# Attention and gated MoE on one core: weight words, least scale and work order moved between engines

## The chip, the cores and the metric

The kernel runs on one core of a Trainium2 chip. The time is the device time of one execution in microseconds (us), and lower is better. Before the change the median of three runs is 902.36 us (901.72 to 904.81). The core has five engines with a queue each: PE multiplies matrices, DVE (VectorE), ACT (ScalarE) and POOL (GpSimd) work on tiles elementwise, and SP issues the DMAs.

## The reference

Four batches of eight heads, 768 positions of 64 numbers, then a gated MoE layer on the 3072 rows of 512 that come out:

```python
q_bits = (np.einsum('bhsd,dk->bhsk', q, proj) > 0)      # 6 bits, a bucket number
mask = q_bucket[:, :, :, None] == k_bucket[:, :, None, :]
scores = scale * np.matmul(q, k.transpose(0, 1, 3, 2))
scores = np.where(mask, scores, -1000000000.0)
attn = softmax(scores)                                  # with 1e-9 in the sum
x = np.matmul(attn, v)  # -> [3072, 512]
return (x @ w_a * (x @ w_b)) @ w_out                    # 512 -> 1536 -> 512
```

## The kernel before

Every fp32 operand is split into two fp16 numbers, hi and lo, and a product is three matmuls (hi*hi, lo*hi, hi*lo). The bucket test is part of the score matmul: 12 columns of marks stand beside the 64 of a key or query.

The scores are worked in 192 tiles of 128 queries by 768 keys. A tile goes through this chain: four matmuls `s` on PE, row maximum `mx` on DVE, `width` on DVE, `bias` on ACT (L1039) or DVE (L1045), exponential `e` on ACT, fp16 cast `a` (the hi half) on DVE, ACT (L1064) or POOL (L1065), the lo half `a` by subtraction on POOL (L1075) or DVE (L1079), one DMA transpose of both into `at` issued by SP (L1085), and 18 matmuls `av` on PE. Eight tiles make half a chunk of 256 rows; 12 chunks make the 3072 rows.

A chunk of x is divided by its sums and scaled by a power of two. The first and the last chunk are turned by PE: the two halves of x are scaled by `xsc` (L1215, POOL or DVE), transposed by PE into `px`, and split into `xT` hi (ACT L1241) and lo (DVE L1244). The ten chunks between go through DMA transposes. Then come the MoE matmuls `ab` (L1292), their product `g` (L1314, DVE), its split (hi L1322 ACT or L1326 DVE, lo L1334 POOL) and the matmuls `o` (L1344).

The weights come in as fp32 words in 18 pieces of 128x1024 (SP, L526), each into one of a few staging buffers `raw_w`, `raw_wo`. DVE takes group maxima (L624, L633), PE spreads them over the partitions, DVE reads the maximum (L585 `al_w`), raises it to at least 2^-14 (L599) and makes a power of two of it (L591, L594). A word is then split with integer steps: its hi part on ACT (L547), its low bits by a read of one byte in eight on ACT (L555), both put together by DVE (L562), which frees the staging buffer, and from that the fp16 hi (ACT L640) and lo (POOL L645 or DVE L649).

The order of everything is written out by hand. Each operation has a number, and the list `ORDER` names them in the order in which they are issued; +10000 or +20000 takes the operation's second or third engine, and a negative number -n puts n warming matmuls (`warm`, L1448) on PE that no result uses. An engine runs its instructions strictly in its own order; a semaphore holds an instruction back until what it reads is there and what it overwrites is done. So the engine of each operation and its place in each queue are set by this list alone.

Of the kernel before, what the change touches and what calls it, by code (L numbers as in the profile page):

```python
# [21 lines left out]
P = 128  # L22
# [21 lines left out]
SUMS = [1, 0]  # L44
# [31 lines left out]
def constants():  # L76
# [16 lines left out]

X_BY_PE = (0, NB * NCH - 1)
# [287 lines left out]
def attention_moe(ctx: ExitStack, tc: tile.TileContext, q, k, v, proj, w_a, w_b, w_out, cst, cst_w, out):  # L382
# [40 lines left out]
    veps = cp.tile([P, NB * NPAIR], F32, tag="veps", name="veps")  # L423
    wcut = cp.tile([P, NG], F32, tag="wcut", name="wcut")
    wone = cp.tile([P, NG + NFQ], F32, tag="wone", name="wone")
    wlow = cp.tile([P, NG], F32, tag="wlow", name="wlow")
    wtop = cp.tile([P, 2], F32, tag="wtop", name="wtop")
    wab = cp.tile([P, NPC, WP], F32, tag="wab", name="wab")
    wab16 = wab.bitcast(F16)
# [1057 lines left out]
```

## Time and profile before

| | before |
|---|---|
| median of three runs | 902.36 us |
| profiled execution | 903.96 us |
| its span | 902.2 us |
| PE busy | 859.0 us, 95% |
| DVE busy | 659.1 us, 73% |
| ACT busy | 544.4 us, 60% |
| POOL busy | 450.7 us, 50% |
| mean granted clock | 0.998 |

The span is the profiled execution without 1.76 us around it. "Busy" is time in an instruction, and a matmul that no result uses counts as well. A share of the whole span mixes two stages here, so the rows below are taken by stretch: the time up to 118.1 us, where the first MoE matmul begins, and the time behind it.

### The profile page before, as it was taken

The page shows a single profiled execution, that of the slowest core. Times are in us where ns is not written, and L with a number is a line of the kernel's source. Part 1 is how long each engine was busy: PE and PEld are TensorE (multiplying, and loading weights), DVE is VectorE, ACT ScalarE, POOL GpSimd, SP SyncE. Part 2 cuts the span into 40 slices and gives each one's busy share as a digit, 9 for nine tenths or more (in the row PEclk, how much of TensorE's full clock was granted, in tenths as well). Part 3 has the DMA queues.
Part 4 walks back from the last instruction along what each step waited for, and adds up shares of the span by engine and source line. Part 5 has one row for each costly group of instructions (what it writes and reads, how often), then busy time and mean ns, then how long its engine had stood idle before and what let it go on. Part 6 is the DMA issues. An engine that isn't in the chain of part 4 may idle for free.

```text
span 902.2 us, 23571 instructions
## 1 busy us (share of the span) xinstructions
PE 859.0 (95%) x9432; PEld 650.6 (72%) x9432; DVE 659.1 (73%) x1593; ACT 544.4 (60%) x1049; POOL 450.7 (50%) x388
## 2 busy tenths in 40 slices
PE   4787799999999999999999999999999999999998
PEld 3565577777777777777777777777777777777775
DVE  6999798988888769777876767777888854752310
ACT  5999799976555566556643555645566545543222
POOL 1478878886544373463533264573453545462111
PEclk9999999999999999999999999999999999999999
DMA  9899999999979999988979688997799966654000
GB/s 322 257 249 255 185 227 234 197 190 217 208 150 164 156 168 187 193 154 170 172 126 151 119 139 176 171 201 156 149 191 169 154 115 119 117 108 71 1 25 24
DMA packets 435950, 147.40 MB, mean 163 GB/s; under 512 B 407552, under 2 KB 428160, under 8 KB 435840
## 3 DMA queue, kind: packets, MB, share of 16 engines
q1 hardware_dynamic: 435840, 145.89, 83.2%
q8 instruction: 74, 1.21, 0.6%
q14 instruction: 36, 0.29, 0.1%
HBM read 37.85 MB, written 6.29 MB: 49 GB/s over the span
## 4 chain that ended last, share of the span: by engine, by line
PE 78%; DVE 4%; DMA 3%; ACT 2%; issue 1%; POOL 0%; ACTq 0%; SPq 0%; DVEq 0%
PE ab L1292 38%; PE o L1344 19%; PE s L1011 11%; PE av L1094 9%; DMA at<-a 2%; DMA qTA_q<-marked 1%; DVE mx L1023 1%; ACT e L1055 1%; DVE xz L1194 1%; DMA vr<-in_v_dram 1%; DVE g L1314 0%; PE b_q L802 0%; ACT raw_w L547 0%; ACT a L1064 0%; PE b_k L802 0%
## 5 line engine op out<-in xcount | busy, mean ns | idle before, releaser
L1292 PE MATMUL ab<-xT,wab 128*128 128x256 f16 x3456 | 407.8, 273 | 1.7 <-DVE g L1314 1.7
L1292 PEld LDWEIGHTS <-wab 128*128 128x128 f16 x3456 | 332.6, 98 | 55.8 <-issue 2.7
L1075 POOL TENSOR_TENSOR a<-e,a 128x768 f16<-128x768 f32 x148 | 249.9, 1693 | 107.9 <-ACT a L1064 53.5
L1055 ACT ACTIVATE e<-s,bias,width 128x768 f32<-128x768 f32 x192 | 189.8, 989 | 68.5 <-DVE bias L1045 58.3
L1334 POOL TENSOR_TENSOR g<-g,g 128x256 f16<-128x256 f32 x144 | 106.8, 742 | 234.9 <-ACT g L1322 151.0
L1344 PE MATMUL o<-wo,g 128*128 128x512 f16 x864 | 209.0, 379 | 0.0
L1023 DVE TENSOR_REDUCE mx<-s 128x1 f32<-128x768 f32 x192 | 181.6, 949 | 29.6 <-PE s L1011 29.0
L1314 DVE SCALAR_TENSOR_TENSOR g<-ab,wlow,a 128x256 f32<-128x256 f32 x132 | 63.5, 481 | 139.4 <-ACT a L1306 126.5
L1306 ACT ACTIVATE a<-ab,wlow 128x256 f32<-128x256 f32 x132 | 62.1, 471 | 158.7 <-PE ab L1292 151.9
L1094 PEld LDWEIGHTS <-at 128*128 128x128 f16 x3456 | 122.4, 98 | 28.2 <-DMA at<-a 9.7
L1344 PEld LDWEIGHTS <-g 128*128 128x128 f16 x864 | 81.2, 98 | 74.3
L1094 PE MATMUL av<-vh,at 128*128 128x64 f16 x2304 | 126.6, 194 | 6.9 <-DMA at<-a 6.9
L1011 PE MATMUL s<-kTA_k,qTA_q 128*128 128x384 f16 x384 | 94.2, 327 | 8.6 <-ACT e L1055 6.6
L1011 PE MATMUL s<-kTB_k,qTB_q 128*128 128x384 f16 x384 | 94.2, 327 | 0.0
L1065 POOL CAST a<-e 128x768 f16<-128x768 f32 x62 | 55.4, 895 | 58.8 <-ACT e L1055 47.9
L1064 ACT CAST a<-e 128x768 f16<-128x768 f32 x89 | 73.6, 829 | 5.8 <-DMA at<-a 4.4
L1094 PE MATMUL av<-vl,at 128*128 128x64 f16 x1152 | 65.3, 194 | 0.0
L1322 ACT CAST g<-g 128x256 f16<-128x256 f32 x102 | 40.9, 401 | 38.9 <-DVE g L1314 33.8
L1039 ACT ACTIVATE bias<-mx,width 128x1 f32<-128x1 f32 x101 | 29.3, 293 | 53.5 <-DVE width L1032 53.2
L1011 PEld LDWEIGHTS <-qTB_q 128*128 128x128 f16 x384 | 37.6, 98 | 25.2 <-issue 0.3
L1011 PEld LDWEIGHTS <-qTA_q 128*128 128x128 f16 x384 | 34.6, 98 | 28.3 <-issue 10.8
L1079 DVE TENSOR_TENSOR a<-e,a 128x768 f16<-128x768 f32 x44 | 42.8, 974 | 5.3 <-ACT a L1064 4.1
(149 smaller groups left out, 821.6 us busy)
## 6 DMA issues: line engine op xcount, KB each, us to landing
rk_k<-in_k_dram SPq DMA_DIRECT2D x16, 384.0 KB, 4.7
vr<-in_v_dram SPq DMA_DIRECT2D x16, 384.0 KB, 4.6
rq_q<-in_q_dram SPq DMA_DIRECT2D x12, 512.0 KB, 4.8
raw_w<-in_moe_w_b_dram SPq DMA_DIRECT2D x12, 512.0 KB, 5.2
raw_w<-in_moe_w_a_dram SPq DMA_DIRECT2D x12, 512.0 KB, 6.0
raw_wo<-in_moe_w_out_dram SPq DMA_DIRECT2D x12, 512.0 KB, 5.7
out_dram<-ob SPq DMA_DIRECT2D x24, 256.0 KB, 2.7
at<-a SPq DMA_TRANSPOSE x192, 4.1
```

Source lines behind the costliest of these rows:

```text
L1011: nc.tensor.matmul(ps.t[:, jj, :HALF], lhsT=x.t[:, uq, :], rhs=y.t[:, h * NT + jj * 3 : h * NT + jj * 3 + 3, :].rearrange("p t x -> p (t x)"),
L1023: lambda: nc.vector.tensor_reduce(out=mx.t[:, u : u + 1], in_=halves(ps.t), axis=AX.XY, op=ALU.max, negate=True),
L1055: lambda: nc.scalar.activation(flat2(e.t), halves(ps.t), AF.Exp, bias=bias.t[:, u : u + 1], scale=width.t[:, u : u + 1], accum_out=sm.t[:, ...
L1064: ("ACT", 0.725, lambda: nc.scalar.copy(out=a2.t[:, 0], in_=e.t), False),
L1065: ("POOL", 0.9, lambda: nc.gpsimd.tensor_copy(out=a2.t[:, 0], in_=e.t), False),
L1075: lambda: nc.gpsimd.tensor_tensor(out=a2.t[:, 1], in0=e.t, in1=a2.t[:, 0], op=ALU.subtract),
L1094: nc.tensor.matmul(av.t[:, u, :], lhsT=at.t[:, a + kt, :], rhs=w.t[:, h, kt, :], start=i == 0, stop=i == 3 * NT - 1,)
L1292: nc.tensor.matmul(pl.t[:, m, :CH], lhsT=wt(m, wi, cc, f), rhs=xt.t[:, :, xi * NC + cc, :], start=i == 0, stop=i == 3 * NC - 1,)
L1306: lambda a=a, pl=pl, gr=gr: nc.scalar.activation(a.t, pl.t[:, 0, :CH], AF.Copy, scale=cuts[:, gr : gr + 1]),
L1314: lambda a=a, g32=g32, pl=pl, gr=gr: nc.vector.scalar_tensor_tensor(out=g32.t, in0=pl.t[:, 1, :CH], scalar=cuts[:, gr + 1 : gr + 2], in1=a ...
L1334: lambda g=g, g32=g32: nc.gpsimd.tensor_tensor(out=g[1].t, in0=g32.t, in1=g[0].t, op=ALU.subtract),
L1344: nc.tensor.matmul(po.t[:, u, :], lhsT=g[gi].t[:, us], rhs=wo[f // 2].t[:, f % 2, wi * DM : (wi + 1) * DM], start=f % per_q == 0 and i == ...
```

## The change

The list `ORDER` is a new one (all 200 lines of it), and some operations get other engines to choose from:

- The low bits of a weight word (ACT) may also be taken on POOL, and the fp16 hi of a word (ACT or DVE) too. Five of the 18 low bits and one of the 18 hi casts go to POOL.
- The group maxima of the weights lie in one tile `wmx` that POOL fills with 2^-14 beforehand. Its last column is never written, so the reduce over the columns gives at least 2^-14, and the nine `max` instructions L599 go.
- `ident16`, the operand of the warming matmuls, is cast by POOL from `ident` instead of loaded; POOL clears `pjk` and `pjq`.
- The absolute sums of V and K heads may be taken by ACT with its accumulator, where DVE took a maximum.
- Counts that differ by engine: bias on ACT 101 to 84 and on DVE 91 to 108, sums and maxima of V and K heads on ACT 12 to 17 and on DVE 20 to 15, hi cast `a` on ACT 89 to 97, on DVE 41 to 42 and on POOL 62 to 53, lo `a` on POOL 148 to 144 and on DVE 44 to 48, x scaling on POOL 2 to 1 and on DVE 2 to 3, warming matmuls 318 to 315.

```diff
-SUMS = [1, 0]
+SUMS = [1, 1]
+    wmx = cp.tile([P, NG + NFQ, NC + 2], F32, tag="wmx", name="wmx")
-    op("SP", DMA_ISSUE, lambda: nc.sync.dma_start(out=ident16, in_=cst_w), -60, w=["ident16"], svc=0.3)
-    op("DVE", 0.1, lambda: nc.vector.memset(pjk, 0.0), -100, w=["pjk"])
+    op("POOL", 0.25, lambda: nc.gpsimd.tensor_copy(out=ident16, in_=ident), -60, ...
+    op("POOL", 0.1, lambda: nc.gpsimd.memset(pjk, 0.0), -100, w=["pjk"])
+    op("POOL", 0.1, lambda: nc.gpsimd.memset(wmx, float(2.0**-14)), -100, w=["wmx"])
...
+            alt=[(
+                "POOL", 1.1,
+                lambda: nc.gpsimd.tensor_scalar(
+                    out=low(), in0=raw.t.bitcast(U8)[:, :, 3], scalar1=1.0 / 32, scalar2=-15.5 / 32,
+                    op0=ALU.mult, op1=ALU.add,
+                ),
+                False,
+            )],
...
-            nc.vector.tensor_scalar(out=al.t, in0=al.t, scalar1=float(2.0**-14), scalar2=None, op0=ALU.max)
             power(sc.t, 0x7F800000, -1, 143 * 8)
...
-            lambda: nc.vector.tensor_reduce(out=mx.t[:, 0:1], in_=mx.t[:, 1:], axis=AX.X, op=ALU.max),
+            lambda: nc.vector.tensor_reduce(out=wmx[:, g, 0:1], in_=wmx[:, g, 1:], axis=AX.X, op=ALU.max),
...
-            alt=[("DVE", 0.6, lambda: nc.vector.tensor_copy(out=hi(), in_=z()), True)],
+            alt=[
+                ("DVE", 0.6, lambda: nc.vector.tensor_copy(out=hi(), in_=z()), True),
+                ("POOL", 1.05, lambda: nc.gpsimd.tensor_copy(out=hi(), in_=z()), False),
+            ],
-    6, 12, 0, 52, 60, 3, 2, 1, 40, 13, 296, 5, 299, 4, 14, 53, 300, 295, 15, 26, 16, 272, 61, 17, 273, 7, 276, 62,
+    1, 4, 5, 6, 7, 2, 13, 0, 53, 41, 61, 8, 297, 300, 301, 14, 9, 3, 296, 10, 274, 15, 16, 10054, 273, 17, 278, 11,
...
```

Three places of the order follow. The first is POOL from its first own instruction up to the first tiles, before (`marked` is the marks of a head pair, `a` and `e` belong to the score tiles):

```order
L441 MEMSET marked 128x16x52
L881 COPY marked<-nB_k_0_146 128x12x64
L881 COPY marked<-nB_q_0_176 128x16x64
L881 COPY marked<-nB_k_2_368 128x12x64
L1065 CAST a_0_0_0_0_0_0_521<-e_0_0_0_0_0_466 128x768
L1065 CAST a_0_0_0_0_0_1_530<-e_0_0_0_0_1_459 128x768
```

And the same place of the changed kernel, whose lines have other numbers (L898 is L881 of before, L568 the low bits, L657 the hi cast, L1083 is L1065):

```order
L446 MEMSET wmx 128x54
L448 MEMSET marked 128x16x52
L441 CAST ident_65<-ident 128x128
L898 COPY marked<-nB_q_0_170 128x16x64
L568 ISA
L568 TENSOR_SCALAR raw_w_1_127<-raw_w_1_127 128x1024
L568 TENSOR_SCALAR raw_w_0_138<-raw_w_0_138 128x1024
L568 TENSOR_SCALAR raw_w_1_153<-raw_w_1_153 128x1024
L898 COPY marked<-nB_k_2_397 128x12x64
L657 CAST wab<-wab 128x2x512
L1083 CAST a_0_0_0_0_0_0_517<-e_0_0_0_0_0_464 128x768
```

Three low bits stand between the copy for q and that for the head pair 2, and one hi cast ahead of the first tile; one copy and one cast of `a` have gone to DVE and ACT.

The second place is ACT at the scores of the sixth to eighth tile, before (`e_0_0_1_...` are tiles of the second half of eight, `raw_w` and `raw_wo` weight words):

```order
L1064 CAST a_0_0_0_1_0_1_917<-e_0_0_1_0_1_872 128x768
L1039 ACTIVATE bias_0_0_451<-mx_0_0_445,width_0_0_448 128x1
L555 ACTIVATE raw_w_0_591<-raw_w_0_591 128x1024
L1055 ACTIVATE e_0_0_1_1_0_961,sm_0_0_460<-s_0_0_1_1_0_867,bias_0_0_451,width_0_0_448 128x768
L1039 ACTIVATE bias_0_0_451<-mx_0_0_445,width_0_0_448 128x1
L1064 CAST a_0_0_0_1_1_0_986<-e_0_0_1_1_0_961 128x768
L1055 ACTIVATE e_0_0_1_1_1_1005,sm_0_0_460<-s_0_0_1_1_1_889,bias_0_0_451,width_0_0_448 128x768
```

The same tiles on ACT in the changed kernel (L1082 is the cast, L1073 the exponential, L562 the low bits, L554 the hi part of a word):

```order
L1082 CAST a_0_0_0_1_0_1_887<-e_0_0_1_0_1_847 128x768
L554 ACTIVATE raw_wo_1_525<-raw_wo_1_525,wsc_734 128x1024
L1073 ACTIVATE e_0_0_1_1_0_923,sm_0_0_465<-s_0_0_1_1_0_841,bias_0_0_460,width_0_0_457 128x768
L562 ACTIVATE raw_w_1_789<-raw_w_1_789 128x1024
L562 ACTIVATE raw_wo_1_525<-raw_wo_1_525 128x1024
L1082 CAST a_0_0_0_1_1_0_969<-e_0_0_1_1_0_923 128x768
L1073 ACTIVATE e_0_0_1_1_1_992,sm_0_0_465<-s_0_0_1_1_1_861,bias_0_0_460,width_0_0_457 128x768
```

The two bias instructions between these tiles are now on DVE, and other weight words stand between the exponentials.

The third place is POOL at the scaling of the first chunk, before (L1215 with the two halves `x_0_0` and `x_0_1`):

```order
L1075 TENSOR_TENSOR a_0_1_0_0_1_1_1679<-e_1_0_0_1_1_1637,a_0_1_0_0_1_1_1679 128x768
L1075 TENSOR_TENSOR a_0_1_0_1_0_0_1716<-e_1_0_1_0_0_1682,a_0_1_0_1_0_0_1716 128x768
L1215 TENSOR_TENSOR x_0_1_1684<-x_0_1_1684,xsc_0_1728 128x512
L1215 TENSOR_TENSOR x_0_0_1304<-x_0_0_1304,xsc_0_1728 128x512
L1075 TENSOR_TENSOR a_0_1_0_1_0_1_1807<-e_1_0_1_0_1_1737,a_0_1_0_1_0_1_1807 128x768
```

And of the changed kernel, where L1093 is L1075 and L1233 is L1215:

```order
L1093 TENSOR_TENSOR a_0_1_0_0_1_0_1631<-e_1_0_0_1_0_1551,a_0_1_0_0_1_0_1631 128x768
L1093 TENSOR_TENSOR a_0_1_0_0_1_1_1673<-e_1_0_0_1_1_1623,a_0_1_0_0_1_1_1673 128x768
L1233 TENSOR_TENSOR x_0_1_1677<-x_0_1_1677,xsc_0_1692 128x512
L1093 TENSOR_TENSOR a_0_1_0_1_0_0_1748<-e_1_0_1_0_0_1679,a_0_1_0_1_0_0_1748 128x768
L1093 TENSOR_TENSOR a_0_1_0_1_0_1_1773<-e_1_0_1_0_1_1686,a_0_1_0_1_0_1_1773 128x768
```

The half `x_0_0` is scaled by DVE now, behind one maximum and one width, and POOL scales `x_0_1` one lo half earlier in its queue.

## Rows read from the trace of the kernel before

**Rows 1.** Stretches: start:end, length, busy of PE, PEld, DVE, ACT, POOL, clock, DMA.

```profile
0.00:118.10 118.10, 85.18 (x1018) 63.53 (x1019) 103.15 (x261) 103.66 (x154) 69.72 (x51) 0.99 1.01 250
24.00:29.00 5.00, 3.57 (x29) 2.16 (x27) 4.73 (x17) 5.00 (x8) 0.00 (x0) 1.00 0.40 111
30.00:118.10 88.10, 69.25 (x857) 51.67 (x855) 80.85 (x191) 83.10 (x134) 66.86 (x44) 0.98 1.07 236
118.10:190.00 71.90, 69.56 (x812) 53.20 (x810) 65.50 (x169) 67.57 (x119) 59.42 (x43) 1.00 1.08 218
```

**Rows 2.** PE's matmuls of line L1292: ns, first and last start.

```profile
L1292 PE MATMUL ab<-xT,wab x3456: 269/273/274, 118.1 to 893.6; 128*128 128x256 f16 x192
```

**Rows 3.** Waits of PE behind 118.1 us: in total, times, longest.

```profile
PE ab L1292 <- DVE g L1314: 1.7, 2, 1.4
```

**Rows 4.** Chain of waits, 60 to 150 us: start, length, what.

```profile
97.92 1.65 POOL a L1075
...
99.89 6.03 DMA at<-a
```

**Rows 5.** Timeline of POOL: start, length, what, [idle before <-releaser].

```profile
31.77 0.85 POOL L881 COPY marked<-nB_k 128x768 f16<-128x768 f16 x1 [13.46 <-ACT nB_k L869]
...
84.99 1.59 POOL L1065 CAST a<-e 128x768 f16<-128x768 f32 x1
...
110.40 2.04 POOL L1215 TENSOR_TENSOR x<-x,xsc 128x512 f32<-128x512 f32 x2
```

**Rows 6.** Timeline of DVE, the last step of the chunk's scale.

```profile
109.73 0.15 DVE L1165 TENSOR_SCALAR xsq<-xsq 128x1 int32<-128x1 int32 x1
```

**Rows 7.** Timeline of SP, the issues of `pj`.

```profile
3.25 1.20 SPq L434 DMA_DIRECT2D pj<-in_proj_dram  x2
```

**Rows 8.** Waits of SP's queue up to 118 us.

```profile
SPq L526 <- DVE al_w L585: 8.4, 1, 8.4
```

**Rows 9.** Lines on ACT, whole span: busy, mean ns | idle before.

```profile
L1064 ACT CAST a<-e 128x768 f16<-128x768 f32 x89 | 73.6, 829 | 5.8 <-DMA at<-a 4.4
...
L1039 ACT ACTIVATE bias<-mx,width 128x1 f32<-128x1 f32 x101 | 29.3, 293 | 53.5 <-DVE width L1032 53.2
...
L555 ACT ACTIVATE raw_w<-raw_w 128x1024 int32<-128x1024 uint8 x12 | 13.6, 1152 | 0.0
...
L640 ACT CAST wab<-wab 128x1024 f16<-128x1024 f32 x11 | 11.5, 1044 | 0.0
...
L738 ACT ACTIVATE nB_k<-rk_k 128x768 bf16<-128x768 f32 x12 | 10.0, 836 | 1.2 <-DMA rk_k<-in_k_dram 1.2
...
L944 ACT ACTIVATE nB_q<-rq_q 128x1024 bf16<-128x1024 f32 x6 | 6.4, 1060 | 1.8 <-DMA rq_q<-in_q_dram 1.0 <-DMA kTB_k<-nB_k 0.8
```

**Rows 10.** Lines on DVE, whole span.

```profile
L1079 DVE TENSOR_TENSOR a<-e,a 128x768 f16<-128x768 f32 x44 | 42.8, 974 | 5.3 <-ACT a L1064 4.1 <-POOL a L1065 0.9
...
L1045 DVE TENSOR_SCALAR bias<-mx,width 128x1 f32<-128x1 f32 x91 | 18.9, 210 | 1.8
...
L1326 DVE TENSOR_REDUCE g<-g 128x256 f16<-128x256 f32 x42 | 17.3, 413 | 2.7 <-PE o L1344 2.2
...
L741 DVE TENSOR_REDUCE mx_v<-vr 128x1 f32<-128x768 f32 x16 | 15.0, 941 | 2.9 <-DMA vr<-in_v_dram 2.9
...
L950 DVE TENSOR_REDUCE qmx_q<-rq_q 128x1 f32<-128x1024 f32 x6 | 7.3, 1209 | 0.0
...
L649 DVE TENSOR_TENSOR wab<-wab 128x1024 f16<-128x1024 f32 x3 | 3.7, 1250 | 0.0
...
L1215 DVE TENSOR_TENSOR x<-x,xsc 128x512 f32<-128x512 f32 x2 | 1.3, 683 | 0.0
```

**Rows 11.** Two lines on POOL: ns min/median/max, first and last start.

```profile
L645 POOL TENSOR_TENSOR wab<-wab x8: 2127/2132/2194, 40.1 to 138.4; 128x1024 f16<-128x1024 f32 x8
...
L1065 POOL CAST a<-e x62: 812/822/1906, 35.3 to 806.1; 128x768 f16<-128x768 f32 x62
```

**Rows 12.** Waits of DVE, 118.1 to 200 us.

```profile
DVE g L1314 <- ACT a L1306: 3.3, 5, 1.1
```

More of the change, by code (lines that the diff above doesn't have):

```diff
@@ L91 @@
 T_ISSUE = 1.4
+K_BY_PE = 4
 X_BY_PE = (0, NB * NCH - 1)
@@ L436, in attention_moe @@
         )
-    op("SP", DMA_ISSUE, lambda: nc.sync.dma_start(out=ident16, in_=cst_w), -60, w=["ident16"], svc=0.3)
-    op("DVE", 0.1, lambda: nc.vector.memset(pjk, 0.0), -100, w=["pjk"])
-    op("DVE", 0.1, lambda: nc.vector.memset(pjq, 0.0), -100, w=["pjq"])
+    op(
+        "POOL", 0.25, lambda: nc.gpsimd.tensor_copy(out=ident16, in_=ident), -60, r=["ident"], w=["ident16"],
+        alt=[("DVE", 0.12, lambda: nc.vector.tensor_copy(out=ident16, in_=ident), True)],
+    )
+    op("POOL", 0.1, lambda: nc.gpsimd.memset(pjk, 0.0), -100, w=["pjk"])
+    op("POOL", 0.1, lambda: nc.gpsimd.memset(pjq, 0.0), -100, w=["pjq"])
+    op("POOL", 0.1, lambda: nc.gpsimd.memset(wmx, float(2.0**-14)), -100, w=["wmx"])
     marked = cp.tile([P, NBLK, P], F16, tag="marked", name="marked")
@@ L567, in to_f32, with w_scale @@
         )
-    def w_scale(mx, sc, cut, one, toks, name, key):
+    def w_scale(g, mx, sc, cut, one, toks, name, key):
         al = buf("sc_al", [P, 1], F32, f"al_{name}", 4)
@@ L579, in w_scale @@
             lambda: nc.tensor.matmul(
-                ps.t[:, 0, :P], lhsT=upper(mx.t[:, 0:1]).to_broadcast([P, P]), rhs=upper(ident), start=True, stop=True
+                ps.t[:, 0, :P], lhsT=upper(wmx[:, g, 0:1]).to_broadcast([P, P]), rhs=upper(ident), start=True, stop=True
             ),
@@ L598, in rest @@
         def rest():
-            nc.vector.tensor_scalar(out=al.t, in0=al.t, scalar1=float(2.0**-14), scalar2=None, op0=ALU.max)
             power(sc.t, 0x7F800000, -1, 143 * 8)
-        op("DVE", 0.46, rest, key, r=[al], w=[(al, "max"), sc])
+        op("DVE", 0.3, rest, key, r=[al], w=[(al, "max"), sc])
         def powers():
@@ L611, in w_scale, with load_group @@
         op("DVE", 0.3 if cut is None else 0.6, powers, key + 2, r=[(al, "max")], w=toks, hold=[al])
-    def load_group(srcs, ats, name, key, afters=((), ())):
+    def load_group(g, srcs, ats, name, key, afters=((), ())):
         raws = []
-        mx = buf("wmx", [P, NC + 1], F32, f"wmx_{name}")
+        mx = f"wmx_{name}"
         for i, src in enumerate(srcs):
@@ L624, in load_group @@
                     lambda raw=raw, cc=cc, h=h: nc.vector.tensor_reduce(
-                        out=mx.t[:, cc + 1 : cc + 2],
+                        out=wmx[:, g, cc + 1 : cc + 2],
                         in_=raw.t[:, h * WP : (h + 1) * WP, 1].bitcast(F32), axis=AX.X, op=ALU.max,
@@ L628, in load_group @@
                     ),
-                    key + i + 0.5 * h, r=[(raw, "raw", h)], w=[(mx, cc)],
+                    key + i + 0.5 * h, r=[(raw, "raw", h), "wmx"], w=[(mx, cc)],
                 )
@@ L664, in w_group @@
         ats = [NF // 2 - NSTG + (2 * g + i) % NSTG for i in range(2)]
-        raws, mx = load_group([src[2 * i * P : 2 * (i + 1) * P] for i in range(2)], ats, f"w{g}", key)
+        raws, mx = load_group(g, [src[2 * i * P : 2 * (i + 1) * P] for i in range(2)], ats, f"w{g}", key)
         sc = buf("wsc", [P, 1], F32, f"wsc{g}")
-        w_scale(mx, sc, wcut[:, g : g + 1], wone[:, g : g + 1], [("wcut", g), ("wone", g)], f"w{g}", key + 2)
+        w_scale(g, mx, sc, wcut[:, g : g + 1], wone[:, g : g + 1], [("wcut", g), ("wone", g)], f"w{g}", key + 2)
         for i, raw in enumerate(raws):
@@ L686, in wo_group @@
         raws, mx = load_group(
-            [w_out[f * 2 * P : (f + 1) * 2 * P] for f in (2 * fq, 2 * fq + 1)], (2 * fq, 2 * fq + 1), f"wo{fq}", key,
+            g, [w_out[f * 2 * P : (f + 1) * 2 * P] for f in (2 * fq, 2 * fq + 1)], (2 * fq, 2 * fq + 1), f"wo{fq}", key,
             [[("words", f)] if f >= NF // 2 - NSTG else [] for f in (2 * fq, 2 * fq + 1)],
@@ L690, in wo_group @@
         sc = buf("wsc", [P, 1], F32, f"wsc{g}")
-        w_scale(mx, sc, None, wone[:, g : g + 1], [("wone", g)], f"wo{fq}", key + 2)
+        w_scale(g, mx, sc, None, wone[:, g : g + 1], [("wone", g)], f"wo{fq}", key + 2)
         op(
@@ L905, in kprep @@
         n = f"k{b}_{hp}"
+        by_pe = b == 0 and hp < K_BY_PE
         A, B = natural(n)
@@ L917, in kprep @@
         split(raw, 2 * NT, sc, [sc], A, B, 0, n, key)
-        turn(B, 2 * NT, tB, key, [(B, "hi"), (B, "lo")], n, None if b else TURN[0])
+        turn(B, 2 * NT, tB, key, [(B, "hi"), (B, "lo")], n, TURN[0] if by_pe else None)
         buckets(tB, 2 * NT, pjk, A, ((ALU.is_le, -HOT), (ALU.is_gt, -HOT)), n, key_b, tag)
-        turn(A, 2 * NT, tA, key_b, [(A, "hi"), (A, "mark")], n, None if b else TURN[1])
+        turn(A, 2 * NT, tA, key_b, [(A, "hi"), (A, "mark")], n, TURN[1] if by_pe else None)
     def qprep(b, c, key, tag, key_b):
```

391 rows, old and new, of the table ORDER are left out of this document.

## The prediction

> **What bounds the kernel now.** I read the stretches first, then PE's MoE line, the chain of waits, the timelines where the chain changes engine, and last the durations by line. The first MoE matmul starts at 118.1 us and the last at 893.6 [rows 2]. Before 118.1 PE is busy for 85.18 of 118.1 us, and a part of that is warming matmuls; behind it, up to 190, 69.56 of 71.9 [rows 1]. So two things count: when the first MoE matmul can start, and how much PE waits behind it. Work on the other engines that comes earlier or later without touching either is worth nothing.
>
> What holds the start back is not one engine. In 30 to 118.1 ACT is busy for 83.10 of 88.1 us, DVE for 80.85, the DMA share is 1.07 and POOL has 66.86 [rows 1]. ACT is the fullest, and the chain runs along it: a cast on ACT, the lo half on POOL at 97.92, the transpose of the sixteenth tile, 99.89 for 6.03 us [rows 4], then x, its scale, done at 109.88 [rows 6], and the two scalings on POOL, 110.40 for 2.04 [rows 5], px, xT, the first ab.
>
> **The change, part by part.** The sums are differences of counts in the two orders, times mean durations.
>
> 1. ACT ahead of xT hi. Four low bits less (4 x 1.152 = 4.61), one hi cast less (1.04), eleven biases less (11 x 0.293 = 3.22); three head sums more (3 x 0.836 = 2.51; their accumulator read lies within 0.2 of it each, 0.6), one q sum more (1.06) and three casts more (3 x 0.829 = 2.49) [rows 9]. -8.87 + 6.66 = -2.2; consecutive instructions overlap by about a tenth of a us and there are nine fewer, so I take -1.8, between -1.3 (all overlaps lost) and -2.2. ACT has 5.0 us idle in 88.1 [rows 1], so nearly all of it shows in when xT hi can be made.
>
> 2. DVE ahead of xT lo. Three head maxima (2.82), a q maximum (1.21), a lo half of a weight (1.25) and six L599 (0.9, at the 0.15 of a one-column step of the same operation) go; eleven biases (2.31), two lo halves (1.95), one scaling (0.68) and some ten small ones (about 1.6, an estimate at 0.15 to 0.2 each) come [rows 6, 10]. About +0.4. DVE's 7.3 us of idle time in the stretch [rows 1] covers that; without cover it would cost 0.4. The nine L599 by themselves are 9 x 0.15 = 1.3 us, off the path but for those ahead of xT lo.
>
> 3. POOL. The five low bits and the hi cast are not in the trace as POOL operations. Lower bound: the one-input cast of 768 columns, median 0.822 [rows 11], times 1024/768, 1.10. Upper bound: the two-input subtraction of the same width, 2.13 [rows 11]. I take 1.1, since each has one input. Three of them stand in POOL's idle time of 13.46 us ahead of 31.77 [rows 5]: 3.3 to 6.4 us fit there. What they gate is L562, which frees the staging buffer. SP waited there 8.4 us for `al_w` [rows 8], the DVE read of the maximum that stood behind an L562, and in 24 to 29 the DMA share is 0.40 [rows 1]. With ACT's low bits gone and DVE's maxima fewer by then, that load leaves some 2 us sooner (an estimate: three head maxima and L599 of 3 us, less small DVE work that comes). Cost nothing; the gain is only worth something if transfers bind later on (rival 1).
>
> 4. The start. The two small loads of `pj` go ahead of K, one load less follows. Neither is in a wait that the chain shows; the first tiles stand behind ACT's copies later, so I put 0; it can cost 1.2 us where K waits for the two issues [rows 7], and gain 0.9 where the first scale of K no longer stands behind a V maximum on DVE [rows 10]. POOL's clears and `ident16` cast lie in POOL's idle start.
>
> 5. The x chain. Before, POOL scales both halves one after the other, 2.04 us, from 110.40, half a us after the scale was ready at 109.88 because of the lo half ahead of it [rows 5, 6]. Now POOL scales one half without that lo half ahead, 1.0 from 109.9, and DVE the other behind a maximum and a width, some 1.3 + 0.68. So px is ready at 111.9 where it was 112.4, -0.5; at most -1.0 (POOL alone), at least 0 where DVE waits for the scores of that maximum.
>
> 6. The chain up to the sixteenth transpose. ACT ahead of the sixteenth exponential is 2 us lighter by the same count, POOL's queue ahead of the sixteenth lo half 1.5 us heavier, which its 21.2 us idle in 30 to 118.1 covers [rows 1]. The lo half that is at 97.92 [rows 4] comes 1.8 to 2 us earlier if the transfers let it.
>
> The start of the first ab is then the later of two: by the chain -1.9 - 0.5 = -2.4, by ACT's own queue -1.8. I take -1.8: 116.3 instead of 118.1.
>
> 7. Behind the start. PE's useful work is the same, so is its order from the 57th tile on. DVE has 5.6 us more to do between xT lo and the maximum of the 46th tile: more biases, two more lo halves (1.95), four casts of g (4 x 0.413 = 1.65), the scales of the weights put together earlier (2.2) [rows 10]. Three tiles later the surplus is 2.6. DVE's idle time in 118.1 to 190 is 71.9 - 65.50 = 6.4 us [rows 1], 3.3 of it waits for ACT's `a` [rows 12], and PE has waited 1.7 us for DVE's g [rows 3]. Queued behind each DVE instruction are the g products that free PE's ab buffers. Most of the surplus fits; I give 0.4 us back, from 0 to 5.6.
>
> 8. Three warming matmuls less, 0.27 us each if like an ab matmul [rows 2]: they filled waiting time, 0.
>
> Sum: -1.8 + 0.4 = -1.4 on the profiled execution of 903.96 (span 902.2 and 1.76 around it), 902.56. That execution lies 1.60 above the median of 902.36, so the forecast for the median is 901.0, between 900.1 and 902.0 by the bounds of term 1 and 0 to 0.9 given back.
>
> A rule on POOL bears on term 3. The row: the same 768-column cast takes 0.822 in the median but 1.59 at 84.99 [rows 5, 11], in a stretch where DVE is nearly always busy. The Trainium skill, GPSIMD Engine Reference (1. Specifications), says POOL shares its SBUF interfaces with VectorE and contends with two-input VectorE instructions; this case's 1.59 agrees with that without proving it. If that were the rule for the moved work, each low bit would be 1.10 x 1.59/0.822 = 2.13, and the result would be rival 3.
>
> **The rivals.**
>
> Rival 1, the lead carries in full: faster. The load that SP held back leaves early and the transfers' idle time at 24 to 29, 5.0 x 0.60 = 3.0 us [rows 1], is used; what the saturated queue does later all moves forward by 3.0, and the scaling gives 0.5. For it: DMA share above 1 from 30 on, the transpose of 6.03 us. Against: ACT's queue is only 1.8 lighter. 902.36 - 3.5 = 898.9.
>
> Rival 2, DVE becomes the bound behind the start: slower. The 5.6 us of term 7 don't fit the idle time, because that time is waits for `a` that move along. Then PE's ab buffers wait 5.6 us for g less the lead of 1.8: 902.36 + 3.8 = 906.2. It decides once DVE's idle time in the 72 us behind the start is under about 1 us. For it: DVE 91% busy there [rows 1]. Against: the surplus has shrunk to 2.6 three tiles later, and two score buffers and the fill of ab work stand between.
>
> Rival 3, the gain doesn't arrive: either POOL's new work takes 2.13 and pushes lo halves and staging back by four times 1.03 us ahead of the sixteenth tile, of which the idle start covers three, or the transfers alone set the sixteenth transpose as before. Then only term 5 is left with the 0.4: 902.36 - 0.5 + 0.4 = 902.3, or with the late lo half up to 903.3.
>
> **How the numbers follow.** Forecast 0.42, rival 1 0.27, rival 2 0.15, rival 3 0.16. About 0.3% (2.7 us) is what a measurement of this kernel can tell from no change, so faster is below 899.65 and slower above 905.07. Faster: 0.23 of rival 1, 0.10 of the forecast (its lead could reach term 6's) and 0.01, 0.34. Slower: 0.13 of rival 2 and 0.02 of the rest, 0.15. The rest, 0.51, is the same. The range from 898.0 to 905.0 leaves out about one in ten on either side: the far end of rival 1 and most of rival 2. The likeliest case's own range is 900.1 to 902.0.
>
> **What would show it.** Right: the first ab at 116 to 116.6, ACT still full up to it, low bits on POOL of about 1.1 us, POOL's scaling of 1.0 beside one on DVE of 0.7, and 0 to 1 us more of PE waiting behind the start. Rival 1 would show a first ab near 114.6 and no DMA gap at 24 to 29; rival 2 DVE over 97% busy in 118 to 190 and PE waiting there for g; rival 3 low bits of 2 us or a sixteenth transpose still landing near 105.9. The forecast is wrong in its working if the first ab moves by 1.8 and the end does not.

## The result: slower, and the profile after

The changed kernel takes 908.12 us in the median of 6 runs (905.56 to 912.24); beside it the kernel before took 902.68 (901.72 to 904.81). The ratio is 1.0061, with a 95% interval of 1.0047 to 1.0074. Forecast were 901.0 and a range up to 905.0: the sign was wrong, and the time lies outside the range. Its profiled execution took 908.25 (span 906.5), that of before 903.96, which is 4.29 us of difference to explain.

The stretches of the kernel after, which answer to [rows 1], with the same columns:

```profile
24.00:29.00 5.00, 3.73 (x30) 2.26 (x28) 4.76 (x19) 4.77 (x7) 0.00 (x0) 1.00 0.77 222
30.00:118.10 88.10, 66.58 (x843) 50.48 (x840) 80.85 (x204) 82.09 (x127) 67.65 (x40) 0.98 1.08 228
118.10:190.00 71.90, 69.26 (x820) 53.14 (x821) 67.37 (x166) 65.30 (x115) 47.00 (x36) 1.00 1.11 217
```

ACT is a little freer ahead of 118.1 (82.09 after 83.10), DVE fuller behind it (67.37 after 65.50), the hole in the transfers at 24 to 29 is half closed (0.77 after 0.40): the load moved as the change intends. PE's MoE line, which answers to [rows 2]:

```profile
L1310 PE MATMUL ab<-xT,wab x3456: 269/273/418, 119.2 to 897.8; 128*128 128x256 f16 x192
```

The first ab came 1.0 us later and not 1.8 earlier, the last 4.2 later; the longest, 418 ns where before had 274, ran at a low clock. Between lies most of the loss. Adding up all of PE's records, ab number 481 of 3456 stood at 238.09 before and at 242.83 after. Of these 4.74 us, 3.89 are idle time of PE (36.59 before, 40.48 after: 1.85 of it ahead of the first ab, 2.04 behind), -0.11 is warming, and 0.95 the same work at a lower clock. Where PE waited behind 118.1, up to 250 us (in total, times, longest), answering to [rows 3]:

```profile
PE ps_k L464 <- ACT nB_k L755: 2.9, 1, 2.9
PE av L1112 <- DMA at<-a: 2.7, 2, 2.5
PE s L1029 <- ACT e L1073: 1.8, 1, 1.8
PE ab L1310 <- DVE g L1332: 0.3, 1, 0.3
```

And before, up to 250 too:

```profile
PE ps_k L457 <- DVE marked L815: 1.0, 1, 1.0
PE s L1011 <- ACT e L1055: 0.8, 2, 0.7
PE s L1011 <- DMA qTA_q<-marked: 0.8, 1, 0.8
PE ps_wo L579 <- DVE wmx_wo L633: 0.7, 1, 0.7
```

Three long waits are new, and none is for g; of the waits before, 3.6 us in all, most are gone. The first in time is the av. The chain of waits of the kernel after shows how it arose; it answers to [rows 4]:

```profile
110.87 0.69 ACT a L1082
...
111.60 1.03 POOL a L1093
112.64 5.50 DMA at<-a
...
118.19 0.70 PE av L1112 x18
```

The timelines of PE, DVE and ACT show the x chain beside it:

```profile
111.16 1.09 PE L1247 MATMUL px<-ident,x 128*128 128x128 f32 x8 [0.90 <-DVE x L1233]
...
118.19 0.35 PE L1112 MATMUL av<-vh,at 128*128 128x64 f16 x6 [2.48 <-DMA at<-a]
...
118.94 0.22 PE L594 MATMUL ps_w<-ident,wmx 128*128 128x128 bf16 x1
119.16 0.71 PE L1310 MATMUL ab<-xT,wab 128*128 128x256 f16 x5
...
110.42 0.68 DVE L1233 TENSOR_TENSOR x<-x,xsc 128x512 f32<-128x512 f32 x1
...
115.42 1.22 DVE L1262 TENSOR_TENSOR xT<-px,xT 128x1024 f16<-128x1024 f32 x1
...
114.36 1.01 ACT L1259 CAST xT<-px 128x1024 f16<-128x1024 f32 x1
```

xT was whole at 115.42 + 1.22 = 116.64, but PE's order has the av of the 21st tile and a transpose `ps_w` ahead of the first ab, and that av's transpose landed at 118.14. Before, that av came behind the first ab, at 119.45; the new list put it ahead. The lead of the x chain ended in a queue behind it. The chain counts POOL's lo half, which that transpose needs, from 111.60; in POOL's timeline it began at 110.45, 0.03 us behind DVE's half of x, and took 2.17 us, where 1.64 is its time undisturbed:

```profile
110.45 2.17 POOL L1093 TENSOR_TENSOR a<-e,a 128x768 f16<-128x768 f32 x1
```

The second place, in the timelines of DVE, POOL, ACT and PE:

```profile
171.93 0.65 DVE L1275 TENSOR_SCALAR wlow<-wone,wtop 128x3 f32<-128x3 f32 x1
172.61 1.56 DVE L1276 TENSOR_TENSOR wlow<-wlow,wcut 128x3 f32<-128x3 f32 x1
174.21 0.60 DVE L1277 COPY wlow<-wcut 128x3 f32<-128x3 f32 x1
174.72 0.94 DVE L1041 TENSOR_REDUCE mx<-s 128x1 f32<-128x768 f32 x1
...
170.42 2.14 POOL L662 TENSOR_TENSOR wo<-wo_y,wo 128x1024 f16<-128x1024 f32 x1
172.50 1.66 POOL L1093 TENSOR_TENSOR a<-e,a 128x768 f16<-128x768 f32 x1
174.10 0.69 POOL L1352 TENSOR_TENSOR g<-g,g 128x256 f16<-128x256 f32 x1
...
176.28 0.99 ACT L1073 ACTIVATE e<-s,bias,width 128x768 f32<-128x768 f32 x1 [2.38 <-DVE bias L1063]
...
177.41 0.48 PE L1029 MATMUL s<-kTA_k,qTA_q 128*128 128x384 f16 x2 [1.78 <-ACT e L1073]
```

The common scales of the weights, five small instructions on at most three columns, took DVE from 171.55 to 174.81 ahead of a maximum; the exponential, and then PE's scores, waited. Each of the three long ones ended within 0.03 us of the POOL instruction that ran beside it; in e5 (below), where POOL ran nothing beside the last of them, that one took 0.17, and before, beside shorter instructions of POOL, the five took 2.6. So much of the 3.3 us hangs on what POOL ran meanwhile. The third place, in the timelines of POOL, ACT and PE:

```profile
229.31 0.83 POOL L898 COPY marked<-nB_k 128x768 f16<-128x768 f16 x1
...
234.96 0.84 ACT L755 ACTIVATE nB_k<-rk_k 128x768 bf16<-128x768 f32 x1 [2.59 <-DMA xT<-xz]
...
235.95 0.23 PE L464 MATMUL ps_k<-ident,mx_k 128*128 128x128 bf16 x1 [2.89 <-ACT nB_k L755]
```

ACT's copy of a K head waits for the transposes of `xz`, with which it shares no data. It shares memory: before, the marks copy of the preceding head pair stood on DVE ahead of the splitting of x, and the new `nB_k` got that pair's buffer (offset 129888 in the kernel before); now it stands on POOL behind it in the list, and the pool of tiles gives the new `nB_k` the buffer of `xz` (offset 132192 in the kernel after).

Last the clock. Stretches of PE after (start:end, length, busy, granted clock, DMA share, GB/s):

```profile
100.50:104.00 3.50, 3.50 (x38) 0.55 1.43 170
...
236.00:240.00 4.00, 4.00 (x37) 0.59 1.13 225
```

And the one of before:

```profile
107.00:110.50 3.50, 3.50 (x30) 0.53 0.98 196
```

0.53 to 0.59 is near half: PE works at 1.2 GHz for most of such a stretch. Before has one behind the start-up, after two, each right behind a place where PE stood idle (av products waiting for a transpose, 1.68 us at 99.96 after and 2.04 at 105.97 before; ps_k's 2.89). What the fall at 236 cost stands in PE's timeline of after, where the same 24 ab took 1.67 us longer in it than ahead of it:

```profile
228.45 2.78 PE L1310 MATMUL ab<-xT,wab 128*128 128x256 f16 x24
...
236.60 4.45 PE L1310 MATMUL ab<-xT,wab 128*128 128x256 f16 x24
```

Seen from the first ab, the 4.74 us are its own 1.02, 2.04 of idle time behind it and some 1.7 of this fall.

### The profile page after: what moved, and what is told of

Same layout as the page of the kernel before. It is cut to its first block, busy times and chain, and to the rows that moved or that the text cites. A ratio compares the mean times of both kernels' runs of the same rounds, so it can differ in the third digit from the quotient of the medians.

```text
span 906.5 us, 23590 instructions
## 1 busy us (share of the span) xinstructions
PE 859.6 (95%) x9429; PEld 652.0 (72%) x9429; DVE 657.4 (73%) x1601; ACT 545.4 (60%) x1044; POOL 445.9 (49%) x384
## 4 chain that ended last, share of the span: by engine, by line
PE 78%; DVE 9%; DMA 5%; issue 3%; ACT 3%; POOL 1%; SPq 0%; ACTq 0%; POOLq 0%; DVEq 0%
PE ab L1310 38%; PE o L1362 18%; PE s L1029 11%; PE av L1112 9%; DMA at<-a 3%; DVE mx L1041 2%; DMA raw_wo<-in_moe_w_out_dram 1%; ACT e L1073 1%; DVE wmx L638 1%; DVE wab L577 1%; ACT a L1082 1%; DVE g L1332 1%; POOL a L1093 1%; DMA xT<-xz 1%; DMA vr<-in_v_dram 0%
## 5 line engine op out<-in xcount | busy, mean ns | idle before, releaser
L1093 POOL TENSOR_TENSOR a<-e,a 128x768 f16<-128x768 f32 x144 | 243.4, 1695 | 120.0 <-ACT a L1082 54.8
L1073 ACT ACTIVATE e<-s,bias,width 128x768 f32<-128x768 f32 x192 | 190.0, 990 | 74.1 <-DVE bias L1063 64.5
L1082 ACT CAST a<-e 128x768 f16<-128x768 f32 x97 | 80.4, 830 | 4.2 <-DMA at<-a 2.9
L1083 POOL CAST a<-e 128x768 f16<-128x768 f32 x53 | 46.9, 886 | 53.0 <-ACT e L1073 47.9
L1057 ACT ACTIVATE bias<-mx,width 128x1 f32<-128x1 f32 x84 | 24.2, 292 | 51.5 <-DVE width L1050 51.4
L1097 DVE TENSOR_TENSOR a<-e,a 128x768 f16<-128x768 f32 x48 | 46.2, 962 | 5.2 <-ACT a L1082 3.9
```

Of the source, the lines that this page charges most:

```text
L1073: lambda: nc.scalar.activation(flat2(e.t), halves(ps.t), AF.Exp, bias=bias.t[:, u : u + 1], scale=width.t[:, u : u + 1], accum_out=sm.t[:, ...
L1082: ("ACT", 0.725, lambda: nc.scalar.copy(out=a2.t[:, 0], in_=e.t), False),
L1083: ("POOL", 0.9, lambda: nc.gpsimd.tensor_copy(out=a2.t[:, 0], in_=e.t), False),
L1093: lambda: nc.gpsimd.tensor_tensor(out=a2.t[:, 1], in0=e.t, in1=a2.t[:, 0], op=ALU.subtract),
```

## The experiments

All were run beside the kernel before (23 or 24 executions of it each time, median 902.88 to 903.43). A trace is that of one execution, which can lie at either end of its kernel's range: e1's took 902.61 us, e4's 907.28. Numbers in the edits are operations of `ORDER`, negative ones warming matmuls; edits are to the changed kernel's list unless said.

**The three waits, one by one and together.** e1 puts the marks copy (1232) back ahead of the split of x, e2 the 21st av (634) behind the first x projections, e3 the common scales of the weights (483) later.

```diff
-778, 1234, 1187, ... 1205, 1232, 1206
+778, 1234, 1232, 1187, ... 1205, 1206
-642, 634, 659, ... 380, 484, 680
+642, 659, ... 380, 484, 634, 680
-544, 483, 900, ... 981, 20959, 935
+544, 900, ... 981, 20959, 483, 935
```

The first pair of lines is e1, the second e2, the third e3; e4 has all three.

> The changed kernel with one entry of the order moved: POOL's marks copy of the key pair k1_2 (L898) is issued ahead of the split of x instead of behind its two transposes. Theory A: the late copy held the nB buffer of k1_2, so the sum of k1_3 on ACT (L755) got the other nB buffer, that of xz, and waited until 234.88 for the transposes; PE's ps_k waited 2.89 us for it and ran at a granted clock of 0.59 for 4 us behind it (0.95 us more). Then the wait is gone and the time is 3.0 to 3.8 us shorter, 904.3 to 905.1 where the changed kernel has 908.1. Rival B: the sum waited for its own data or for a late SP queue, and the buffer is a coincidence: ps_k still waits 2 to 3 us, time 908 within 1.

Measured: 906.43 (900.49 to 910.87), ratio 1.0036 [1.0014, 1.0058]. In its trace ps_k waits 0.29:

```profile
231.64 0.23 PE L464 MATMUL ps_k<-ident,mx_k 128*128 128x128 bf16 x1 [0.29 <-ACT nB_k L755]
```

The wait was the buffer, as the addresses said; by the medians against before it was worth 2.1 us (+5.44 to +3.36), though the intervals of e1 and of the changed kernel overlap and 3.0 to 3.8 were expected.

> The changed kernel with one entry moved: the av matmuls of the 21st tile (L1112) are issued behind the first 24 ab matmuls instead of ahead of them. Theory A: xT was whole at 116.64, 1.1 us earlier than in the kernel before, but PE's order had that av ahead of the first ab, and its transpose landed at 118.14; so the first ab now starts near 116.8 instead of 119.2 and the time is 2.0 to 2.4 us shorter, 905.7 to 906.1. Rival B: the rest of PE's work is not ready earlier, and what the first ab gains is waited for in the 30 us behind it: 0 to 0.8 us shorter. Rival C: the weights of the first ab (wab) or ps_w hold it as well: first ab at 118 or later.

Measured: 907.39 (905.64 to 909.13), 1.0054 [1.0041, 1.0068]. The first ab came at 118.5 and not at 116.7, since px was late in that execution and ps_w waited 1.2 us for an exponential. The gain is not clear of noise.

> The changed kernel with one entry moved: the common scale of the weights on DVE (one_scale, L1271 to L1277, 171.55 to 174.81) goes some 20 us later in DVE's queue, to about where the kernel before has it. Theory A: the maximum of the 44th tile stood behind it, so its exponential came 2.38 us late and PE's s waited 1.78 us at 177.4; then that wait is gone and the time is 1.3 to 1.8 us shorter, 906.3 to 906.8. Rival B: DVE has no idle time in 118 to 200, so the 3.3 us fall on another tile or on g: within 0.5 of 908.1, and the wait of 1.78 comes again later.

Measured: 907.50 (904.06 to 910.96), 1.0054 [1.0034, 1.0074]. The wait of the scores was gone and two others had come, in PE's timeline:

```profile
196.17 0.48 PE L1029 MATMUL s<-kTA_k,qTA_q 128*128 128x384 f16 x2 [0.93 <-ACT e L1073]
201.52 0.22 PE L464 MATMUL ps_k<-ident,mx_k 128*128 128x128 bf16 x1 [2.21 <-DVE marked L832]
```

> The changed kernel with the three moves of the marks copy, the av and the common scale together. If the three waits are independent the gains add: 3.4 + 2.2 + 1.5 = 7.1 us shorter than 908.1, so 901.0, 1.7 below the kernel before. If they share a cause (transfers or DVE as the one bound behind the start) the sum is 4 us or less: 904 or above.

Measured: 903.02 (901.90 to 909.13), 1.0011 [0.9996, 1.0025]. Together they take nearly all of the loss away; alone e2 and e3 take almost none, within overlapping intervals. The lead did not appear: level with before, not faster. The trace does not show why the median fell: that execution, with 907.28 one of the longer ones, had its first ab at 121.52 and a wait of 2.3 us at ps_k.

**Nearby versions.** e5 is e4 with 483 moved less far (behind 1106) and ps_w (397) behind the first x projections; e7 is e5 with 483 left where the change has it.

> The changed kernel with the marks copy and the av moved as before, and two more moves: PE's ps_w for the sixth weight group goes behind the first 12 ab matmuls (ahead of them it waited 1.21 us for a score buffer in the run of the three moves), and the common scale of the weights stands behind the lo half of the key pair k1_0 on DVE (about 186 us) instead of at 195, where PE's ps_k of k1_1 came to wait 2.32 us. Theory A (single waits in PE's order, each worth what it shows): first ab right behind xT lo, 1.2 us gained there and up to 2.3 at ps_k, median 903.0 - 2 = 901, between 899.5 and 902. Rival B (DVE is full from 118 to 200, so the 3.3 us of the common scale cost 1.8 to 2.3 wherever they stand): only the 1.2 us, 901.8 to 903, with a wait of PE of about 2 us behind 186.

> The changed kernel with the marks copy, the av and the ps_w moved, and the common scale left where the change has it. Theory A: PE's 1.8 us of waiting at 177 stay, against 2.3 at ps_k in the kernel of the three moves, and the ps_w wait of 1.2 goes: 903.0 - 1.2 - 0.5 = 901.3. Rival B (DVE's load elsewhere decides): equal to the kernel of the three moves, 903.

Measured: e5 903.53 (901.72 to 909.53), 1.0008 [0.9992, 1.0025]; e7 904.66 (901.54 to 906.78), 1.0013 [0.9999, 1.0027]; both lie above what either theory had. In e7's profiled run (903.12) the start had its lead and more, 115.39 where before had 118.14:

```profile
115.39 1.48 PE L1310 MATMUL ab<-xT,wab 128*128 128x256 f16 x12
```

and its last ab came at 892.69, 0.93 ahead of before's: 1.8 of the 2.75 had been given back.

**The ACT term by itself.** e6 is e4 with the five low bits back on ACT (10315 to 315, and four more alike).

> The kernel of the three moves with the five low bits back on ACT (L562) and none on POOL. Theory A (ACT's queue sets xT, the forecast's first term): four of the five stand ahead of xT hi on ACT at 1.04 each, so xT is whole 3 to 4 us later and the median is 905.5 to 907 where the three moves have 903.0. Rival B (the transfers or POOL set the start, and POOL's low bits contend with DVE): within 1 of 903.0, or below it.

Measured: 909.31 (908.07 to 915.43), 1.0076 [1.0054, 1.0098]. In an order built for POOL's low bits, their 5.8 us on ACT cost 6.3 (909.31 - 903.02; 5.9 with each taken against before), more than the 905.5 to 907 expected: ACT's queue does bear on the start, the prediction's first term. In the trace, that of the longest run (915.43), a second delay adds to it, which follows below e10.

**A bias behind long DVE work.** In e4's profiled run ACT waited 5.30 us at 78.67 for a bias that stood on DVE behind two weight words. e8 is e7 and e9 is e5 with that width and bias moved ahead of both words; e10 is the changed kernel with this alone.

```diff
-210, 182, 339, ... 334, ... 366, 211, 10212, 10173
+210, 211, 10212, 182, 339, ... 334, ... 366, 10173
```

> The kernel with the marks copy, the av and the ps_w moved, and one more move: width and bias of the 11th tile on DVE (L1050, L1063) go right behind that tile's maximum, ahead of the two weight combines (L577) instead of behind them. Theory A: ACT's exponential stood behind the two combines by way of that bias, 2.4 us in a quiet run and 5.3 us where POOL's two-input work stretched the combines from 1.21 to 1.96 and 2.66 us; that is why single executions of the changed kernel scatter over 8 us. Then ACT's wait at 75 us is under 0.5, xT is whole 2 us earlier, the scatter shrinks to some 3 us and the median is 901 to 902 where that kernel had 904.7. Rival B: the scatter comes from the transfers and the granted clock in the start; then the wait goes but the median stays within 1 of 904.7 and the scatter stays.

> The same with the common scale at about 186 us as well: the five moves together. PE's 1.8 us at 177 then become about 1.9 us at 189, as in the run of the four moves, so within 0.5 of the run without that move; 901 to 902 by theory A, 903 to 904 by rival B.

> The changed kernel with width and bias of the 11th tile moved alone. Theory A: the start gains up to 2 us as far as the av ahead of the first ab lets it (its transpose must come earlier too), the other waits stay: 906 to 907 where the changed kernel has 908.1, with less scatter. Rival B: no difference, 908 within 1.

Measured: e8 906.90, 1.0033 [1.0018, 1.0048]; e9 906.73, 1.0040 [1.0026, 1.0054]; e10 909.99, 1.0082 [1.0064, 1.0100]. Each is slower than its parent by 1.9 to 3.2 (e9 clear of e5 by the intervals, the other two not). This theory fell.

A collision that the change brought along shows when the traces are laid side by side. POOL scales one half of x and DVE the other, and a lo half `a` stands on POOL right behind its half. In seven traces (after, e1 to e5, e7) DVE's half began 0.01 to 0.03 us ahead of that lo half: DVE's half took 0.68, and xT was whole 7.35 us behind the start of the scaling. In the seven others (e6, e8 to e12, e15) the lo half began 0.05 to 0.15 ahead: DVE's half took 2.04 to 2.13, ACT then waited 1.4 to 1.5 for a bias behind it, and xT was whole after 8.7 to 10.2. Before, with both halves on POOL, it took 7.31. The lines on DVE and POOL in e11:

```profile
110.17 2.04 DVE L1233 TENSOR_TENSOR x<-x,xsc 128x512 f32<-128x512 f32 x1
...
110.02 1.64 POOL L1093 TENSOR_TENSOR a<-e,a 128x768 f16<-128x768 f32 x1
```

So the traces of e8 to e10 lost 1.4 us there that their parents' did not, and that of e6 2.5. Each is one execution; that all runs of these kernels do so is not shown.

**The clock.** Most of the reordered kernels scatter over 5 to 11 us, the kernel before over 3 to 4, and a run's time goes with its mean granted clock: six runs of e7 at 0.998 took 901.54 to 903.67, six at 0.996 or 0.997 took 905.66 to 906.78. A mean clock lower by 0.002 is worth 1.8 us of 902, less than half of the 4 between the two groups. Cause or sign? e11 is the changed kernel with 44 warming matmuls ahead of four waiting av products, e12 e7 with 40, e13 the kernel before with 39 fewer.

```diff
- 123, ... 208, ... 217, ... 244
+ -12, 123, ... -11, 208, ... -9, 217, ... -12, 244
- 187, -15, ... 215, -11, ... 10358, -16, ... -5, 607, ... -6, 616
+ 187, -5, ... 215, -3, ... 10358, -6, ... 607, ... 616
```

The first pair is e11, the second e13.

> The changed kernel with 44 more warming matmuls (some 0.11 us each, 4.8 us in all), put in PE's order right ahead of four av products that waited for their transposes in its trace (at 66.14 for 1.78 us, 88.24 for 1.59, 91.94 for 1.27, 99.96 for 1.68), so that PE works where it stood idle. Nothing else differs. Theory C (the clock is a cause: the changed start leaves PE idle in such places, the granted clock falls to 1.2 GHz for stretches of about 3 us, and this makes the time longer and scatter): fewer such stretches before 120 us, a higher mean clock, the range of the runs narrower than 906 to 912, median 904 to 906. Rival W (the clock only follows the waits; the 5 us are the three waits in the order): 907.5 to 909, the range as wide as before, the waits of one_scale, of the 21st av and of ps_k as they were.

> The kernel of e7_noscale (marks copy back ahead of xz's split, 21st av and its ps_w behind the first x projections; 904.66, runs in two clusters, 901.5 to 903.7 and 905.7 to 906.8) with 40 more warming matmuls right ahead of four av products that waited in its trace (66.38 for 1.86 us, 88.78 for 1.88, then the av behind it, and 104.88 for 1.19). Theory C: the upper cluster goes, median 901 to 902.5, that is 1 to 2 us faster than the kernel before, which would be the fastest version. Rival W: 904 to 905, still two clusters; if the warming itself delays what stands behind it, 905 to 906.

> The kernel before with 39 of its warming matmuls left out between 81 and 99 us (15 to 5, 11 to 3, 16 to 6, and two groups of 5 and 6 whole), nothing else. No product depends on them. Theory C: the granted clock falls oftener there, runs scatter over some us as those of the changed kernel do, median 904.5 to 907. Rival W: 902.5 to 903.5 as before, within 0.1%; the waits decide, and fewer warming matmuls take nothing from the end.

Measured: e11 904.00 (902.70 to 909.58), 1.0022 [1.0009, 1.0035], well apart from the changed kernel's 1.0061; e12 903.61 (900.26 to 908.50), 1.0011 [0.9995, 1.0027]; e13 906.01 (902.75 to 907.21), 1.0034 [1.0022, 1.0045]. Work without any product gained 4.3 us against before (+5.44 to +1.12), and leaving such work out cost the kernel before 3.1. One stretch of PE in e13:

```profile
86.00:92.00 6.00, 5.25 (x49) 0.51 1.06 197
```

Stretches of PE in e11:

```profile
80.00:105.00 25.00, 20.63 (x267) 1.00 1.15 217
...
113.00:116.50 3.50, 3.50 (x25) 0.52 0.71 136
...
236.00:240.00 4.00, 4.00 (x31) 1.00 0.97 237
```

e13's clock is at 1.2 GHz from 86 to 92, where before's was whole; but this execution is one of its shorter ones (903.71), with the first ab at 115.94 and ab 481 at 238.21, so it does not show where the median's 3.1 went. e11 lost the falls at 100 and 236, but has one at 113, and the range of its runs did not narrow as expected. Its ab 481 stood at 237.87 and not at 242.83: 6.77 less idle, 4.87 more warming, 3.06 less for the same work. The first ab came at 119.23, as late as after's; the gain lies behind it. With the order as it was, the 21st av found its transpose there and ps_k waited 0.7 for `nB_k` and not 2.9; of the three waits only that behind the scales, 1.7, stayed. So e11 does not part the clock from the waits. e12 is 1.05 below e7 (0.5 with each taken against before), which the intervals do not tell from nothing, where 2.2 to 3.7 were looked for. So, is the fall taken away, or moved? e14 puts 33 warming matmuls ahead of three waiting av products of the kernel before (11 ahead of 207, 7 of 225, 15 of 261), e15 35 into e5 (13, 15 and 7 ahead of 123, 217 and 262).

> The kernel before with 33 more warming matmuls right ahead of the three av products that waited longest in its own trace (89.31 for 1.57 us, 94.16 for 1.11, 105.97 for 2.04; behind the last of them its clock fell to 1.2 GHz from 107.0 to 110.5). Theory C (what e11 and e13 showed of the start holds here too): that stretch goes or comes rarer, 901.3 to 902.4, that is 0.5 to 1.5 us under the kernel before. Rival R (the warming only moves the fall to a later place, as e11's profile had one at 113.0 to 116.4 and e12's one at 103.7 to 107.2): 902.5 to 903.5.

> The kernel of e5_four (the changed kernel with all four places of the order undone; 903.53, 901.7 to 909.5) with 35 more warming matmuls ahead of three av products that waited in its trace (66.35 for 1.94 us, 91.42 for 2.35, 107.19 for 1.13). Theory C: both causes are taken out, the lead of the changed start arrives: 900.5 to 902.3, faster than the kernel before by up to 2 us. Rival R (the fall of the clock only moves, as in e12, which gained 1 us of 1.8 looked for): 902.5 to 904.

Measured: e14 905.56 (902.33 to 906.41), 1.0017 [1.0006, 1.0027]; e15 903.40 (898.89 to 910.30), 1.0009 [0.9987, 1.0030]. Moved, in the one trace: e14's has its fall at 103.5 to 107.1, before's was at 107.0 to 110.5, and warming that was more than the idle time it filled (4.49 against 3.10) put ab 481 0.8 us later, at 238.89. The median rose by more, 2.3, and that is worse than either theory had it. e15 has the shortest single run of all, 898.89, and others up to 910.30. No version beats the kernel before: e4, e5, e7, e12 and e15 are level with it within their intervals.

## Why the prediction was wrong

**The step that failed first: "The start of the first ab is then the later of two".** The sum took the x chain and ACT's queue, and left out a third term, PE's own order, in which an av and a ps_w stand ahead of the first ab, the av by the change itself. xT was whole 1.07 us earlier in the profiled run (116.64 after 117.71) and 1.85 in e1's, somewhat less than term 1's 1.3 to 2.2 in the one and within it in the other, and ACT had no idle time right ahead of its part of xT: the first term was about right. The first ab came 1.02 later; in e7's trace, where the av and the ps_w stand behind it, 2.75 earlier, though in e5's, with the same order there and a later x, only 0.43. Term 6 speaks of the sixteenth transpose, and that landed at 105.42 after 105.92, 0.5 earlier and not 1.9; the one that counted was the twenty-first.

Term 5 gained nothing. x was ready at 111.1 after 112.4 (the "at most -1.0 (POOL alone)" is a slip: by the term's numbers POOL alone has x at 110.9, 1.5 earlier), but xT was whole 7.35 us behind the start of the scaling after 7.31, for ACT came to it 2.1 us behind px. And DVE's half stretched the lo half of the 21st tile by 0.5 us, so its transpose, for which the av waited, left that much later.

**Term 7, mis-sized and with the wrong mechanism.** Given back were 0.4, up to 5.6 if DVE made PE's ab wait for g. That wait did not grow: 1.7 over the whole span as in [rows 3], and 0.3 after none up to 250 us; and DVE's own waits for `a`, 3.3 in [rows 12], shrank to 0.4 up to 200 us. DVE was busy for 94% in 118 to 190, so rival 2's mechanism did not happen; that its time, 906.2, is the nearest of the four is luck. What PE lost behind the start was 2.04 of idle time and some 1.7 of clock, at two places: five small instructions ahead of one maximum, and the buffer, with the fall of the clock behind it. The scales, put at 2.2 without a row, took 3.26; and the parts that the term prices add up to 5.8 ahead of its biases, not to 5.6. The first was in the order for whoever followed each DVE instruction to the tile that waits behind it; the forecast only counted their total. The second the order does not show at all.

**What the forecast did not hold: the clock.** PE's idle time in the start was put at nothing (term 8: "they filled waiting time, 0"). It is also where the granted clock falls. e11 and e13 show from both sides that warming in these places is worth 3 to 4 us in the median; that it acts by way of the clock is not shown, since e11's trace lost two of the waits as well and e13's is that of one of its shorter runs. How much of the changed kernel's 5.4 is the three waits and how much the clock cannot be added up: e4 undoes the three places and gains 4.5 us by its ratio (0.0050 lower), e11 leaves the order as it is and gains 3.5 (0.0039). Each changes the other, since the falls come behind waits. Why a given run has more falls than the next stays open.

**What held.** Three of the five low bits on POOL take the lower bound of term 3, one took 1.70 and one 2.01; the hi cast and the single scaling are as forecast. The lines on POOL (ns min/median/max, first and last start), answering to [rows 5, 11]:

```profile
L568 POOL TENSOR_SCALAR raw_w<-raw_w x4: 1102/1133/1704, 17.6 to 57.6; 128x1024 int32<-128x1024 uint8 x4
...
L568 POOL TENSOR_SCALAR raw_wo<-raw_wo x1: 2007/2007/2007, 132.1 to 132.1; 128x1024 int32<-128x1024 uint8 x1
...
L657 POOL CAST wab<-wab x1: 1044/1044/1044, 30.5 to 30.5; 128x1024 f16<-128x1024 f32 x1
...
L1233 POOL TENSOR_TENSOR x<-x,xsc x1: 1042/1042/1042, 109.3 to 109.3; 128x512 f32<-128x512 f32 x1
```

and the durations on ACT (busy, mean ns | idle before), answering to [rows 9], are unchanged, so the counts were worth what was put:

```profile
L1082 ACT CAST a<-e 128x768 f16<-128x768 f32 x97 | 80.4, 830 | 4.2 <-DMA at<-a 2.9
L1057 ACT ACTIVATE bias<-mx,width 128x1 f32<-128x1 f32 x84 | 24.2, 292 | 51.5 <-DVE width L1050 51.4
...
L562 ACT ACTIVATE raw_w<-raw_w 128x1024 int32<-128x1024 uint8 x8 | 9.2, 1153 | 0.0
```

Term 4, the early load of `pj`, cost nothing that shows: its two issues stand at the head of the chain now, 1.15 us, but the first av came at 43.91 after 43.82. Term 8, "0" for three fewer warming matmuls, holds for their number, though one takes 0.11 us of PE and not 0.27 (44 took 4.87 in e11); e13 shows that a matmul that only fills waiting time is not worth 0 as such. Rival 1 had its sign (the hole at 24 to 29 closed by half) and not its result, since the lead stopped at the av. Rival 3's contention is there, but not where the rival put it: against the median of each line POOL's instructions ahead of 120 us were stretched by 5.9 us in all, 2.8 before; on the way to the first ab it was the 0.5 of one lo half.

## What to carry to other kernels

A lead on a chain is worth only what the instructions ahead of its last step in that engine's own queue let through: follow each of them to its inputs. Where an order is written out, a tile's buffer depends on which earlier tile was last read, so moving a reader can make two unrelated tensors wait for each other; compare the addresses of before and after. Where two engines are to share a step, look at what each runs beside it: here POOL and DVE stretch one another, and which of the two begins first decides who pays. Where an engine idles in a stage, take the clock as part of the price of every new wait, and judge versions by many runs.

## What the runs showed of the hardware

The granted clock falls to about half, 1.2 GHz, for 3.5 us, in e13 for 6, behind idle places of PE (1.68 us at 99.96 and 2.89 at 235.95 after, 2.04 at 105.97 before, 2.48 at 112.26 in e11); not every such place has one, the 2.48 us at 118.19 after has none. With warming matmuls put into them the fall was gone or stood elsewhere, in one trace each.

POOL and DVE stretch one another, and the one that begins first keeps its time. DVE's scaling of half of x took 0.68 in seven traces where it began first, and POOL's lo half 2.17 where 1.64 is normal; in the seven where POOL's began first DVE's took 2.04 to 2.13. The line on DVE in e6, where PE waited 2.41 us for it:

```profile
118.58 2.13 DVE L1233 TENSOR_TENSOR x<-x,xsc 128x512 f32<-128x512 f32 x1
```

An instruction on three columns is stretched as well: 1.56 us beside POOL's lo half at 172.50 in the kernel after, where the one behind it in e5 took 0.17 with nothing on POOL. POOL's lo half of a weight took 2.90 us at 66.82 in the kernel after, where 2.13 is normal.
